# Seven half-block products in place of eight in the second FFN product of chunks 2 to 8 (sliding-window attention, then a gated FFN, one core)

## The chip, the core and the metric

The kernel runs on one core of a Trainium2 chip. The time is device microseconds of one execution. Before the change the median of three runs is 325.51 us (325.38 to 325.64). PE is TensorE's matmul, PEld its weight load, DVE VectorE, ACT ScalarE, POOL GpSimd, SP the engine whose queue issues most DMAs.

## What is computed

```
q, k, v: (8, 8, 576, 64)      # batch, heads, tokens, head width
scores = q k^T / 8, masked: heads 0-3 "plain" (0 <= i-j < 32),
         heads 4-7 "dilated" (0 <= i-j < 128 and (i-j) % 4 == 0)
attn   = softmax(scores) v    # (8, 8, 576, 64)
x      = attn, heads side by side: (4608, 512)
out    = (gelu(x w_gate) * (x w_val)) w_out      # d_ff = 1536, out (4608, 512), float32
```

## The kernel before

The FFN runs over 9 chunks c of 512 tokens. A chunk has two stages, and each is written out as a string of words (`gate_words`, `out_words`, lines 910 to 962) that `run_program` (L853) turns into instructions: the order on every engine's queue is the order of the words. A number n takes the next n matmuls from the stage's list.

*Gate stage.* For each of the 12 blocks nb of d_ff (128 wide) 4 matmuls of 512 columns for the gate and 4 for the value (`ffn1_part`, L623), into two PSUM banks; `g` (L872) is the gelu on ACT, `u` (L877) the product with the value on DVE, which reads the second bank, scales by USCALE and writes `u_all[:, nb]` in fp16. The banks alternate: 0 and 7 for even nb, 1 and 4 for odd. `firsts` (L970) gives the order of the first 16 matmuls by hand, since the xT of this chunk (the attention output, transposed, in four pieces kc) is only just ready. `F`, `H` and `R` load, cast (POOL) and turn (DMA transpose) q, k and v of a later batch; `e3` evicts the last output block of the chunk before.

*Output stage.* In chunks 0 to 6 the second product is plain (`ffn2`, L630): for each of 4 token blocks 12 matmuls of 128x512, in banks 0 and 7 alternately, each evicted by `w` (DVE, L643) or `e` (ACT, L641) with the scale 1/USCALE and sent by a DMA of SP (L645). Between these matmuls stands the attention of batch c+1, in four units i, j, k, l of two heads each: `S` scores (L458), `P` exp on ACT (L488), `M` mask on DVE (L493), `D` denominators and `N` numerators on PE (L458), `l` and `r` log and reciprocal on ACT (L585, L591), `X` the division on DVE, which writes xT (L614). S, D and N use stretches of banks 1 to 6 again and again, so each waits for the reader of what was there. `v0` and `v1` are POOL's casts of a later v (L254), held behind the masks. `E` and `G` load ACT's tables.

*Seven products.* In chunks 7 and 8 (`SEVEN`, L822) the second product is one level of a Strassen-like scheme: tokens in two halves, w_out's columns in two halves, and the 12 blocks of d_ff in 6 pairs give 2x2 blocks, and 7 products of such blocks replace 8. A product is 12 matmuls of 256 columns (`products`, L696). It needs sums of u (`u_sums`, L664 to 672, three per pair j: `k{j}@0` to `@2`) and of weights (`weight_sums`, L651 to 660, five per third of w_out, done in chunk 6: `K`). `part_out` (L708) takes a snapshot of the accumulating bank (q0, q1, q3 on ACT or DVE into `snap`) or an output block (q2, q4, q5, q6), and `part_sum` (L736 to 740) adds snapshots to each other, on POOL in chunk 7 and DVE in chunk 8. `last_products` (L747) does the last product of chunk 8 in three pieces.

Of the kernel before, what the change touches and what calls it, by code (L numbers as in the profile page):

```python
# [17 lines left out]
USCALE = 16.0  # L18
# [3 lines left out]
def kernel(  # L22
# [70 lines left out]
    t3s = [xT[i][:, 0:CH].rearrange("p (j d) -> p j d", j=2) for i in range(3)]  # L93
# [553 lines left out]
    def weight_sums(i, part):  # L647

        w = wo_t[i].rearrange("p (j k) (h d) -> p j k h d", k=2, h=2)
        b11, b12, b21, b22 = (w[:, :, k, h] for k in range(2) for h in range(2))  # L650
        if part == 0:  # L651
            nc.vector.tensor_tensor(wx[i][:, 0], b11, b22, ALU.add)
        elif part == 1:
            nc.vector.tensor_tensor(wx[i][:, 1], b11, b12, ALU.add)
        elif part == 2:
            nc.vector.scalar_tensor_tensor(wx[i][:, 2], b21, -1.0, b22, ALU.mult, ALU.subtract)
        elif part == 3:
            nc.vector.tensor_tensor(t3s[i], b12, b22, ALU.subtract)
        else:
            nc.vector.tensor_tensor(wx[i][:, 3], b21, b11, ALU.subtract)  # L660

    def u_sums(j, part):

        k0, k1 = u_all[:, 2 * j, :], u_all[:, 2 * j + 1, :]  # L664
        if part == 0:
            nc.vector.tensor_tensor(ux[:, j, 1:3].rearrange("p s t -> p (s t)"), k0, k1, ALU.add)
        elif part == 1:
            nc.vector.tensor_tensor(ux[:, j, 0], k0[:, 0:256], k1[:, 256:512], ALU.add)
        else:
            two = u_all[:, 2 * j : 2 * j + 2, :]  # L670
            flat = two.rearrange("p k t -> p (k t)")[:, 256:768].rearrange("p (k t) -> p k t", k=2)
            nc.vector.tensor_tensor(flat, two[:, :, 256:512], two[:, :, 0:256], ALU.subtract)

    def operands(kind):

        found = []
        for j in range(NKP):
            w = wo_t[j // 2][:, 2 * (j % 2) : 2 * (j % 2) + 2]
            x, k0, k1 = wx[j // 2][:, :, j % 2], u_all[:, 2 * j], u_all[:, 2 * j + 1]
            found.append(  # L680
                {
                    1: (ux[:, j, 0], x[:, 0]),
                    2: (ux[:, j, 2], w[:, 0, 0:HM]),
                    3: (k0[:, 0:256], t3s[j // 2][:, j % 2]),
                    4: (k1[:, 256:512], x[:, 3]),
                    5: (ux[:, j, 1], w[:, 1, HM:DM]),
                    6: (k0[:, 256:512], x[:, 1]),
                    7: (k1[:, 0:256], x[:, 2]),
                }[kind]
            )  # L690
        return found

    def products(bank, kind, first):

        return [
            lambda s=s, t=t, p=p, st=first and j == 0 and p == 0, end=j == NKP - 1: nc.tensor.matmul(  # L696
                ps[:, bank, HM * p : HM * p + HM], s[:, P * p : P * p + P], t, start=st, stop=end, skip_group_check=True
            )
            for j, (s, t) in enumerate(operands(kind))
            for p in range(2)  # L700
        ]

    def seven(banks):

        order = ((1, 3, True), (0, 4, True), (1, 5, False), (0, 1, False), (1, 2, True), (0, 7, False), (1, 6, True))
        return [mm for b, kind, first in order for mm in products(banks[b], kind, first)]

    def part_out(c, what, eng, banks):  # L708

        src, by = ps[:, banks[0 if what in (1, 3, 5) else 1], :], 1.0 / USCALE  # L710
        m3, a, f = snap
        dst = {0: m3, 1: a, 3: f}.get(what)
        osb = None
        if dst is None:
            osb = osbp.tile([P, DM], F32, tag="osb")
            dst = osb
        if what < 4:
            if eng:
                nc.scalar.activation(dst, src, AF.Copy, bias=0.0, scale=by)  # L719
            else:  # L720
                nc.vector.tensor_scalar(dst, src, by, None, ALU.mult)
        else:
            other, op = {4: (a, ALU.add), 5: (m3, ALU.subtract), 6: (f, ALU.add)}[what]
            nc.vector.scalar_tensor_tensor(dst, src, by, other, ALU.mult, op)  # L724
        if osb is not None:
            tiles["O", what] = osb
            t0, d0 = c * CH + 256 * (what in (4, 6)), HM * (what in (2, 6))
            dram = out[t0 : t0 + 256, d0 : d0 + HM].rearrange("(p r) d -> r p d", r=P)
            nc.sync.dma_start(out=dram, in_=osb.rearrange("r (p d) -> r p d", p=2))

    def part_sum(what, eng):

        m3, a, f = snap
        e = nc.vector if eng else nc.gpsimd
        if what == 0:
            e.tensor_tensor(f, f, m3, ALU.add)  # L736
        elif what == 1:
            e.tensor_tensor(m3, tiles["O", 2], m3, ALU.subtract)
        else:
            e.tensor_tensor(f, f, tiles["O", 4], ALU.subtract)  # L740

    def last_products(c):

        for p, c0, c1, bank in ((0, 0, HM, 3), (1, 0, P, 5), (1, P, HM, 6)):
            for j, (s, t) in enumerate(operands(6)):
                src = ps[:, bank, 0 : c1 - c0]
                nc.tensor.matmul(src, s[:, P * p : P * p + P], t[:, c0:c1], start=j == 0, stop=j == NKP - 1)  # L747
            osb = osbp.tile([P, DM], F32, tag="osb")
            dst, rest = osb[:, 0 : c1 - c0], snap[2][:, HM * p + c0 : HM * p + c1]
            nc.vector.scalar_tensor_tensor(dst, src, 1.0 / USCALE, rest, ALU.mult, ALU.add)  # L750
            t0 = c * CH + 256 + P * p
            (nc.scalar if c0 else nc.sync).dma_start(out=out[t0 : t0 + P, HM + c0 : HM + c1], in_=dst)
# [69 lines left out]
    SEVEN = range(7, NCH)  # L822
# [30 lines left out]
    def run_program(c, words, mms, banks):  # L853
# [3 lines left out]
        for word in words.split():  # L857
# [16 lines left out]
            elif kind == "u":  # L874
                nb = args[0]
                val = ps[:, gate_banks(c, nb)[1], :]
                nc.vector.scalar_tensor_tensor(u_all[:, nb, :], tiles.pop(("g", nb)), USCALE, val, ALU.mult, ALU.mult)  # L877
# [5 lines left out]
            elif kind == "K":  # L883
                weight_sums(*args)
            elif kind == "q":
                part_out(c, args[0], args[1], banks)
            elif kind == "s":
                part_sum(*args)
            elif kind == "L":
                mms.clear()  # L890
                last_products(c)
            elif kind == "V":
                (second, second_v)[args[0] if args else 0]()
            elif kind == "v":
                cast_part(c + 2, args[0], tiles["M"])
            elif kind == "F":
                load_first(args[0])
            elif kind == "H":
                load_rest(args[0])
            elif kind == "R":  # L900
                load_rest(3)
                load_first(4)
                load_rest(4)
            elif kind == "E":
                nc.scalar.preload_act_table_set("natural_log_exp_and_others")
            else:
                nc.scalar.preload_act_table_set("gelu_and_others")  # L907
        assert not mms

    def gate_words(c):  # L910
# [10 lines left out]
        if c in SEVEN:  # L921
            for j in range(NKP - 1):
                sums[2 * j + 1] += f" k{j}@0 k{j}@1 k{j}@2"
        if c == min(SEVEN) - 1:
            for i in range(3):
                for part in range(5):
                    sums[1 + (5 * i + part) * 2 // 3] += f" K{i}@{part}"
# [3 lines left out]
        before = f"e3@{c - 1}" if c < NCH - 1 and c - 1 not in SEVEN else ""  # L931
        last = f" u{NNB - 1} k5@0 k5@1 k5@2" if c > 6 else ""
        return f"{before} {loads} 7 G 3 g0 1 u0 1 g1 4 u1{sums[1]} {rest} 4 g{NNB - 1} 4{last}"

    def out_words(c):
# [6 lines left out]
        if c > 6:  # L942
            tail = "12 q6@0" if c < NCH - 1 else "L"
            return f"12 q0@1 12 q1@1 12 q2@0 12 q3@1 s0@{c - 7} s1@0 12 q4@0 s2@{c - 7} 12 q5@0 {tail}"
        i, j, k, l = (NHP * (c + 1) + n for n in range(NHP))
        v0, v1 = (" v0", " v1") if 2 < c < 6 else ("", "")
        if c in SEVEN:
            ahead = c > 2
            open_ = f"E P{i} P{j} 1 u11" if ahead else f"1 u11 7 S{i}@1+S{j}@4 E P{i} P{j}"
            after = f"S{l + 1}@12+S{l + 2}@15" if 1 < c < 6 else ""  # L950
            return (
                f"{open_} k5@0 k5@1 {11 if ahead else 4} q0@0 M{i} M{j}{v0} k5@2 12 q1@1 8 S{k}@1+S{l}@4 D{i}@11+D{j}@41 4 q2@0 "
                f"P{k} P{l} M{k} M{l}{v1} 12 q3@0 s0@0 s1@0 l{i} l{j} r{i} r{j} 12 q4@0 s2@0 N{i}@10+N{j}@40 D{k}@12+D{l}@42 "
                f"X{i} X{j} 12 q5@0 6 l{k} r{k} l{l} r{l} N{k}@13+N{l}@43 {after} X{k} 6 q6@0 X{l}"
            )
        first = f"1 u11 4 S{i}@1+S{j}@4 E P{i} P{j} M{i} M{j} 7 w0 5" if c < 3 else f"E P{i} P{j} 1 u11 M{i} M{j}{v0} 12 w0 3"
        after = f"S{l + 1}@12+S{l + 2}@15" if 1 < c < 6 else ""
# [12 lines left out]
    firsts = {c: orders[c if c < 3 else 2 if c == 3 else 3] for c in range(NCH)}  # L970
# [37 lines left out]
```

## Time and profile before

| | |
|---|---|
| median of 3 runs | 325.51 us |
| profiled execution | 325.92 us |
| its span, first to last instruction | 324.2 us |
| mean granted TensorE clock | 0.998 |
| gate stage of chunks 2 to 8, each (L623, 96 matmuls) | 20.72 us |
| output stage of chunk 2 / 3 to 5 / 6 / 7 | 14.07 / 13.3 / 12.91 / 9.17 us |

The page of the profile gives the busy time of each engine, the chain of work that ended last followed back from the end, and the costliest groups of instructions. In a row of the timeline or the groups stand start (us), duration (us), engine, line, operation, out<-in, shape, count, and in brackets the idle time of the engine before it and what ended it. A row of the chain has start, duration, engine, line and count. Matmul ends are modelled, and a row of several matmuls runs to the end of the last; neighbours overlap in it. A busy engine that nobody waits for costs nothing, so the chain is read first.

### The profile page before, as it was taken

The page shows a single profiled execution, that of the slowest core. Times are in us where ns is not written, and L with a number is a line of the kernel's source. Part 1 is how long each engine was busy: PE and PEld are TensorE (multiplying, and loading weights), DVE is VectorE, ACT ScalarE, POOL GpSimd, SP SyncE. Part 2 cuts the span into 40 slices and gives each one's busy share as a digit, 9 for nine tenths or more (in the row PEclk, how much of TensorE's full clock was granted, in tenths as well). Part 3 has the DMA queues.
Part 4 walks back from the last instruction along what each step waited for, and adds up shares of the span by engine and source line. Part 5 has one row for each costly group of instructions (what it writes and reads, how often), then busy time and mean ns, then how long its engine had stood idle before and what let it go on. Part 6 is the DMA issues. An engine that isn't in the chain of part 4 may idle for free.

```text
span 324.2 us, 7943 instructions
## 1 busy us (share of the span) xinstructions
PE 317.5 (98%) x3273; PEld 162.6 (50%) x3273; DVE 173.6 (54%) x287; ACT 159.1 (49%) x239; POOL 87.7 (27%) x138
## 2 busy tenths in 40 slices
PE   7999999999999999999999999999999999999995
PEld 4754544444544454445444454445444544684474
DVE  6764646435543355436543554446676467636654
ACT  2673567434653557347633764366535753333320
POOL 8785703402491422231124111411000000040001
PEclk9999999999999999999999999999999999999999
DMA  8999997998899898898389627973000210021003
GB/s 190 183 198 207 205 192 154 268 185 193 194 253 207 214 198 237 191 223 183 126 191 242 161 78 178 249 169 111 32 3 0 92 42 0 0 84 47 2 1 129
DMA packets 107700, 47.11 MB, mean 145 GB/s; under 512 B 83600, under 2 KB 104080, under 8 KB 107664
## 3 DMA queue, kind: packets, MB, share of 16 engines
q1 hardware_dynamic: 94160, 38.29, 51.1%
q0 software_dynamic: 12944, 7.67, 16.6%
q10 hardware_dynamic: 560, 0.66, 0.7%
q8 instruction: 25, 0.41, 0.5%
q14 instruction: 11, 0.09, 0.1%
HBM read 37.75 MB, written 9.44 MB: 146 GB/s over the span
## 4 chain that ended last, share of the span: by engine, by line
PE 92%; DMA 4%; DVE 1%; POOL 1%; issue 0%; DVEq 0%
PE ps L623 58%; PE ps L630 23%; PE ps L458 6%; PE ps L696 5%; DMA wg<-in_moe_w_gate_dram 2%; DMA xT<-in_q_dram 2%; POOL xT L182 0%; DVE turned L740 0%; PE ps L378 0%; DVE osb L724 0%; PE ps L398 0%; DVE osb L750 0%; POOL band L123 0%; DVE ones L67 0%; PE ps L447 0%
## 5 line engine op out<-in xcount | busy, mean ns | idle before, releaser
L877 DVE SCALAR_TENSOR_TENSOR u_all<-g,ps 128x512 f16<-128x512 f16 x108 | 74.2, 688 | 93.3 <-PE ps L623 76.2
L872 ACT ACTIVATE g<-ps 128x512 f16<-128x512 f32 x108 | 63.6, 597 | 105.3 <-PE ps L623 105.3
L623 PE MATMUL ps<-xT,wg 128*128 128x512 f16 x432 | 112.5, 379 | 0.2 <-DMA wg<-in_moe_w_gate_dram 0.2
L623 PE MATMUL ps<-xT,wv 128*128 128x512 f16 x432 | 112.3, 379 | 0.0
L630 PE MATMUL ps<-wo,u_all 128*128 128x512 f16 x336 | 77.8, 380 | 0.0
L623 PEld LDWEIGHTS <-wv 128*128 128x128 f16 x432 | 42.1, 98 | 51.0 <-DMA wv<-in_moe_w_val_dram 0.6
L623 PEld LDWEIGHTS <-wg 128*128 128x128 f16 x432 | 42.1, 98 | 50.5 <-DMA wg<-in_moe_w_gate_dram 0.3
L630 PEld LDWEIGHTS <-u_all 128*128 128x128 f16 x336 | 30.8, 98 | 35.6 <-issue 0.5
L614 DVE TENSOR_TENSOR xT<-ps,rb 128x576 f16<-128x576 f32 x32 | 28.7, 936 | 16.2 <-PE ps L458 12.9
L488 ACT ACTIVATE P<-ps 128x832 f16<-128x832 f32 (+1 forms) x32 | 25.3, 835 | 15.8 <-PE ps L458 15.7
L217 POOL CAST s<-stage 128x640 f16<-128x640 f32 x24 | 17.3, 747 | 53.5 <-DMA stage<-in_q_dram 38.9
L254 POOL CAST v<-stage 128x1152 f16<-128x1152 f32 x11 | 13.0, 1184 | 62.0 <-DMA stage<-in_v_dram 43.5
L585 ACT ACTIVATE lg<-ps 128x576 f32<-128x576 f32 x30 | 18.7, 653 | 11.4 <-DVE xT L614 8.8
L591 ACT ACTIVATE rb<-lg 128x576 f32<-128x576 f32 x30 | 19.5, 690 | 0.3
L736 POOL TENSOR_TENSOR turned<-turned,vdiag 128x512 f32<-128x512 f32 x1 | 1.3, 1262 | 65.6 <-ACT turned L719 65.6
L229 POOL CAST s<-stage 128x512 f16<-128x512 f32 x24 | 14.4, 629 | 8.6 <-DMA stage<-in_q_dram 6.7
L643 DVE TENSOR_SCALAR osb<-ps 128x512 f32<-128x512 f32 x21 | 14.4, 685 | 2.6 <-PE ps L630 2.0
L493 DVE TENSOR_TENSOR P<-P,two_p 128x832 f16<-128x832 f16 x14 | 8.6, 612 | 10.9 <-ACT P L488 10.9
L493 DVE TENSOR_TENSOR P<-P,two_d 128x768 f16<-128x768 f16 x14 | 9.1, 664 | 9.8 <-ACT P L488 9.2
L907 ACT ACT_TABLE_LOAD x9 | 11.5, 1283 | 0.2
L458 PEld LDWEIGHTS <-v 64*64 64x64 f16 x616 | 7.7, 107 | 6.2 <-issue 5.1
L458 PEld LDWEIGHTS <-q 64*64 64x64 f16 x576 | 7.9, 107 | 5.3 <-issue 3.7
(90 smaller groups left out, 208.0 us busy)
## 6 DMA issues: line engine op xcount, KB each, us to landing
out_dram<-osb SPq DMA_DIRECT2D x35, 256.0 KB, 2.2
stage<-in_v_dram SPq DMA_DIRECT2D x28, 144.0 KB, 3.6
stage<-in_q_dram SPq DMA_DIRECT2D x24, 128.0 KB, 3.6
stage<-in_k_dram SPq DMA_DIRECT2D x24, 128.0 KB, 2.9
stage<-in_q_dram SPq DMA_DIRECT2D x6, 512.0 KB, 5.1
stage<-in_k_dram SPq DMA_DIRECT2D x6, 512.0 KB, 5.3
stage<-in_v_dram SPq DMA_DIRECT2D x20, 128.0 KB, 2.9
wo<-in_moe_w_out_dram POOLq DMA_DIRECT2D x3, 512.0 KB, 16.2
```

Source lines behind the costliest of these rows:

```text
L217: nc.gpsimd.tensor_copy(s16[:, 1280 * t + 640 * g : 1280 * t + 640 * g + 640].rearrange("p (k c) -> p k c", k=5), st_of(i).rearrange("p (k ...
L458: nc.tensor.matmul(o[cols], lhs[rows], rhs[rows], start=st, stop=end, skip_group_check=True)
L488: nc.scalar.activation(pt[:, 0 : src.shape[1]], src, AF.Exp, bias=0.0, scale=scale)
L493: tiles["M"] = nc.vector.tensor_tensor(pt, pt, mask, ALU.mult)
L585: nc.scalar.activation(lg, psf[:, c0 : c0 + S], AF.Ln)
L591: nc.scalar.activation(rb, tiles.pop(("lg", n)), AF.Exp, scale=-1.0)
L614: nc.vector.tensor_tensor(dst, num, rb, ALU.mult)
L623: nc.tensor.matmul(ps[:, bank, :], w[:, kc, ns], xT[kc][:, tok], start=first, stop=end)
L630: nc.tensor.matmul(ps[:, bank, :], u_all[:, fc, tb * P : (tb + 1) * P], wo_t[fc // 4][:, fc % 4, :], start=(fc == 0), stop=(fc == NNB - 1),)
L696: lambda s=s, t=t, p=p, st=first and j == 0 and p == 0, end=j == NKP - 1: nc.tensor.matmul(ps[:, bank, HM * p : HM * p + HM], s[:, P * p : ...
L872: nc.scalar.activation(g, ps[:, gate_banks(c, args[0])[0], :], AF.Gelu)
L877: nc.vector.scalar_tensor_tensor(u_all[:, nb, :], tiles.pop(("g", nb)), USCALE, val, ALU.mult, ALU.mult)
```

## The change

The seven products are used in chunks 2 to 8 instead of 7 and 8. They follow another scheme of the same kind: product 1 (first in order) takes u and w_out as they are, there are four sums of u per pair in three operations (the first writes two), of which those after the first can cover two pairs at once, four sums of weights per third, and the snapshots are no longer added to each other: q0, q1, q2 are snapshots, q3, q4, q5 evictions that add one snapshot, q6 a plain eviction. u of odd blocks is stored negated in these chunks and USCALE is 8. The fourth weight sum lies in `wx` rather than in a free part of xT. Weight sums are made in chunk 1.

```
-USCALE = 16.0
+USCALE = 8.0
...
+    def u_sums(j, part, n=1):
+        lo, hi = slice(0, 2 * P), slice(2 * P, 4 * P)
         if part == 0:
+            k0 = u_all[:, 2 * j, :].rearrange("p (h t) -> p h t", h=2)
+            nc.vector.tensor_tensor(ux[:, j, 0:2], k0, u_all[:, 2 * j : 2 * j + 2, hi], ALU.subtract)
+            return
+        at = slice(j - n + 1, j + 1)
+        k0, k1 = (u_all.rearrange("p (j k) t -> p j k t", k=2)[:, at, k] for k in range(2))
+        if part == 1:
+            nc.vector.tensor_tensor(ux[:, at, 2], k0[:, :, lo], ux[:, at, 1], ALU.subtract)
         else:
+            nc.vector.tensor_tensor(k0[:, :, hi], ux[:, at, 2], k1[:, :, lo], ALU.subtract)
...
+    ORDER = ((0, 1, True), (1, 7, True), (0, 6, False), (1, 4, False), (0, 5, False), (1, 2, True), (0, 3, False))
...
+        if what in (3, 4, 5):
+            add = snap[{3: 2, 4: 1, 5: 0}[what]]
+            nc.vector.scalar_tensor_tensor(dst, src, -by if what == 5 else by, add, ALU.mult, ALU.add)
+        elif eng:
+            nc.scalar.activation(dst, src, AF.Copy, bias=0.0, scale=by)
+        else:
+            nc.vector.tensor_scalar(dst, src, by, None, ALU.mult)
+        if final:
+            sent(c, what, dst)
```

(`dst`, `src` and `add` with their reshapes left out here.) `ORDER` gives the place (0 or 1 of the stage's two banks), the product and whether it opens the bank: in chunks 2 to 6 place 0 is bank 0, place 1 bank 7. So q0, q2, q4, q6 read bank 0 and q1, q3, q5 bank 7, and each product but the fresh ones adds to a bank that the eviction before it must have read. `sent` issues the DMA of one 256x256 block, from SP unless told otherwise.

The last chunk gets a function of its own, in which products 1, 6, 5 and 3 go to two banks (one for each half of 128 tokens), 7 and 4 to a third, and the end is in pieces:

```
+        run(two, 1, True)
+        part_out(c, 0, 1, both)
+        run(z, 7, True)
+        part_out(c, 1, 1, 5)
+        run(two, 6, False)
+        part_out(c, 2, 1, both)
+        run(z, 4, False)
+        part_out(c, 3, 0, 5)
+        run(two, 5, False)
+        part_out(c, 4, 0, both)
+        run([(6, 0)], 2, True, parts=((0, 0, 256),))
+        piece(5, c11, ps[:, 6, 0:HM], 0, 0, 256)
+        run([None, (4, 0)], 2, True, parts=((1, 0, 128),))
+        piece(5, c11, ps[:, 4, 0:P], 1, 0, 128)
+        for p in range(2):
+            run(two, 3, False, parts=((p, 0, 256),))
+            piece(6, c12, ps[:, 2 + p, 0:HM], p, 0, 256, act=True)
+        run([None, (0, -P)], 2, True, parts=((1, P, 256),))
+        piece(5, c11, ps[:, 0, 0:P], 1, P, 256, q=nc.scalar)
```

The words (a number is matmuls; in `q0@1` the 1 stands for ACT, 0 for DVE; `k1@1@2` covers two pairs):

```
-    SEVEN = range(7, NCH)
+    SEVEN = range(2, NCH)
...
+                sums[2 * j + 1] += f" k{j}@0" + (f" k{j}@1@2 k{j}@2@2" if j % 2 else " k4@1 k4@2" if j == 4 else "")
...
+        before = "" if c == NCH - 1 else f"q6@1@{c - 1}" if c - 1 in SEVEN else f"e3@{c - 1}"
+        first = "7 G 1 g0 2 u0 4 g1 2 u1" if c - 1 in SEVEN and c < NCH - 1 else "7 G 3 g0 1 u0 1 g1 4 u1"
...
+            return "12 q0@1 12 q1@1 12 q2@1 12 q3@0 12 q4@0 12 q5@0 12 q6@1" if c < NCH - 1 else "L"
...
+            if c == 2:
+                open_ = f"1 u11 k5@0 7 S{i}@1+S{j}@4 E P{i} P{j} k5@1 4 q0@0 k5@2 M{i} M{j} 12 q1@1 6"
+            else:
+                open_ = f"E P{i} P{j} 1 u11 k5@0 k5@1 11 q0@0 k5@2 M{i} M{j}{v0} 12 q1@1 8"
             return (
+                f"{open_} S{k}@1+S{l}@4 D{i}@11+D{j}@41 P{k} P{l} {6 if c == 2 else 4} q2@0 M{k} M{l}{v1} 12 l{i} l{j} r{i} r{j} q3@0 "
+                f"12 N{i}@10+N{j}@40 D{k}@12+D{l}@42 q4@0 X{i} l{l} X{j} l{k} r{l} r{k} 12 q5@0 {8 if c == 2 else 4} "
+                f"N{k}@13+N{l}@43 {after} X{l} X{k} {4 if c == 2 else 8}"
             )
...
+    orders[4] = "012 013 112 113 002 003 001 000 011 010 102 103 101 100 111 110"
+    orders[5] = "010 011 110 111 000 001 003 002 013 012 100 101 103 102 113 112"
+    firsts = {c: orders[c if c < 3 else 3 if c == NCH - 1 else 4 if c == 3 else 5] for c in range(NCH)}
```

`q6` of chunks 2 to 6 stands at the head of the next chunk's gate stage, where `e3` stood, with its output DMA ahead of that stage's loads. A word of `orders` is block, gate (0) or value (1), and kc: the new orders begin with the value matmuls of blocks 0 and 1, in banks 7 and 4, and reach bank 0 with the fifth. Chunks 0 and 1 keep their words but for the weight sums in chunk 1's gate stage.

More of the change, by code (lines that the diff above doesn't have):

```diff
@@ L691, in operands @@
         return found
[L693 to L697, printed above, removed]
-            )
[L699 to L718, printed above, removed]
+    def products(banks, kind, first, parts=((0, 0, 256), (1, 0, 256))):
+        mms = []
+        for j, (s, t) in enumerate(operands(kind)):
+            opened = set()
+            for p, c0, c1 in parts:
+                bank, at = banks[p]
+                o = ps[:, bank, at + c0 : at + c1]
+                st, end = first and j == 0 and bank not in opened, j == NKP - 1
+                opened.add(bank)
+                mms.append(
+                    lambda o=o, s=s[:, P * p : P * p + P], t=t[:, c0:c1], st=st, end=end: nc.tensor.matmul(
+                        o, s, t, start=st, stop=end, skip_group_check=True
+                    )
+                )
+        return mms
@@ new lines, with seven, sent @@
+    ORDER = ((0, 1, True), (1, 7, True), (0, 6, False), (1, 4, False), (0, 5, False), (1, 2, True), (0, 3, False))
+    def seven(banks):
+        return [mm for b, kind, first in ORDER for mm in products([(banks[b], 0), (banks[b], HM)], kind, first)]
+    def sent(c, what, tile, p=slice(0, 2), cols=slice(0, 256), eng=None):
+        t0, d0 = c * CH + 256 * (what in (3, 4)), HM * (what in (4, 6))
+        dram = out[t0 : t0 + 256, d0 : d0 + HM].rearrange("(p r) d -> r p d", r=P)
+        (eng or nc.sync).dma_start(out=dram[:, p, cols], in_=tile.rearrange("r (p d) -> r p d", p=2)[:, p, cols])
@@ new lines, in part_out @@
+    def part_out(c, what, eng, src):
+        src, by = ps[:, src, :] if isinstance(src, int) else src, 1.0 / USCALE
+        final = what > 2
+        dst = osbp.tile([P, DM], F32, tag="osb", name="part") if final else snap[what]
+        if what in (3, 4, 5):
+            add = snap[{3: 2, 4: 1, 5: 0}[what]]
+            nc.vector.scalar_tensor_tensor(
+                dst.rearrange("r (p d) -> r p d", p=2) if len(src.shape) > 2 else dst,
+                src,
+                -by if what == 5 else by,
+                add.rearrange("r (p d) -> r p d", p=2) if len(src.shape) > 2 else add,
+                ALU.mult,
+                ALU.add,
+            )
+        elif eng:
+            nc.scalar.activation(
+                dst.rearrange("r (p d) -> r p d", p=2) if len(src.shape) > 2 else dst, src, AF.Copy, bias=0.0, scale=by
+            )
+        else:
+            nc.vector.tensor_scalar(dst, src, by, None, ALU.mult)
+        if final:
+            sent(c, what, dst)
@@ L719, in part_out, with last_chunk, run, piece @@
+    def last_chunk(c):
+        by = 1.0 / USCALE
+        two = [(2, 0), (3, 0)]
+        both = ps[:, 2:4, 0:HM]
+        z = [(5, 0), (5, HM)]
+        def run(banks, kind, first, **kw):
+            for mm in products(banks, kind, first, **kw):
+                mm()
+        def piece(what, osb, src, p, c0, c1, act=False, q=None):
+            dst = osb[:, HM * p + c0 : HM * p + c1]
+            if act:
                 nc.scalar.activation(dst, src, AF.Copy, bias=0.0, scale=by)
             else:
[L721 to L752, printed above, removed]
+                nc.vector.scalar_tensor_tensor(dst, src, -by, snap[0][:, HM * p + c0 : HM * p + c1], ALU.mult, ALU.add)
@@ new lines, in piece @@
+            sent(c, what, osb, slice(p, p + 1), slice(c0, c1), q)
+        run(two, 1, True)
[8 more added lines that the diff above has]
+        part_out(c, 4, 0, both)
+        c11 = osbp.tile([P, DM], F32, tag="osb", name="c11")
+        c12 = osbp.tile([P, DM], F32, tag="osb", name="c12")
+        run([(6, 0)], 2, True, parts=((0, 0, 256),))
@@ L885, in run_program @@
             elif kind == "q":
-                part_out(c, args[0], args[1], banks)
-            elif kind == "s":
-                part_sum(*args)
+                what, eng, at = (args + [c])[:3]
+                part_out(at, what, eng, out_banks(at)[what in (1, 3, 5)])
             elif kind == "L":
                 mms.clear()
-                last_products(c)
+                last_chunk(c)
             elif kind == "V":
@@ L930, in gate_words @@
             return f"{loads} 8 G 3 g0 1 u0 3 g1 1 u1{sums[1]} {rest} 4 g{NNB - 1} 4"
-        before = f"e3@{c - 1}" if c < NCH - 1 and c - 1 not in SEVEN else ""
+        before = "" if c == NCH - 1 else f"q6@1@{c - 1}" if c - 1 in SEVEN else f"e3@{c - 1}"
         last = f" u{NNB - 1} k5@0 k5@1 k5@2" if c > 6 else ""
-        return f"{before} {loads} 7 G 3 g0 1 u0 1 g1 4 u1{sums[1]} {rest} 4 g{NNB - 1} 4{last}"
+        first = "7 G 1 g0 2 u0 4 g1 2 u1" if c - 1 in SEVEN and c < NCH - 1 else "7 G 3 g0 1 u0 1 g1 4 u1"
+        return f"{before} {loads} {first}{sums[1]} {rest} 4 g{NNB - 1} 4{last}"
     def out_words(c):
```

50 lines of the change are left out of this document (15 added, 35 removed).

## The prediction

> **What bounds the kernel now.** I read the page first (busy shares, chain by engine), then the chain of waits in order of time, the windows of single stages, and the timeline around the hand-overs of PSUM banks.
>
> ```profile
> span 324.2 us, 7943 instructions
> PE 317.5 (98%) x3273; PEld 162.6 (50%) x3273; DVE 173.6 (54%) x287; ACT 159.1 (49%) x239; POOL 87.7 (27%) x138
> PE 92%; DMA 4%; DVE 1%; POOL 1%; issue 0%; DVEq 0%
> ```
>
> TensorE is busy for 98% of the span and 92% of the chain is its own work, so what counts is how long TensorE's list of matmuls is and whether anything makes it wait. The chain gives chunk 5 as one gate stage and one output stage; then come the last attention block of chunk 6 and chunk 7's output stage, which has the seven products already:
>
> ```profile
> 192.78 20.72 PE ps L623 x96
> 213.50 3.45 PE ps L630 x16
> 216.96 0.85 PE ps L458 x64
> 217.81 2.91 PE ps L630 x13
> 220.72 0.87 PE ps L458 x63
> 221.60 3.13 PE ps L630 x14
> 224.72 0.90 PE ps L458 x79
> 225.62 1.19 PE ps L630 x5
> ...
> 258.75 0.50 PE ps L458 x43
> ...
> 281.16 9.17 PE ps L696 x84
> ```
>
> No piece of another engine stands between these rows: the output stage of chunk 5 (13.31 us) is matmuls throughout. A full-width matmul costs 20.72/96 = 215.8 ns, a half-width one 9.17/84 = 109.2 ns. The L630 rows add up to 10.68 us for 48 matmuls against 48 x 215.8 = 10.36; the other 0.32 is the restart after three attention blocks, about 0.11 each (2.91 - 13 x 0.2158).
>
> ```profile
> 213.50:226.81 13.31, 13.31 (x258) 6.85 (x256) 7.59 (x12) 8.98 (x13) 2.29 (x2) 1.00 0.49 134
> 192.78:213.50 20.72, 20.72 (x98) 9.37 (x96) 8.45 (x12) 9.14 (x15) 5.41 (x9) 1.00 0.81 195
> ```
>
> The columns are sum, PE, PEld, DVE, ACT, POOL, granted clock, DMA share, GB/s. The granted clock is full. VectorE has 7.6 of 13.3 us in the output stage and 8.5 of 20.7 in the gate stage. So the change can gain only by shortening TensorE's list, and can lose it again where VectorE or ScalarE, which get more to do, empty a bank late.
>
> **The shorter list.** In chunks 2 to 6 the 48 full-width matmuls of a chunk (10.36 us) become 84 half-width ones (9.17 us): 1.19 us less. Attention blocks and restarts are as many as before. Five chunks: -5.95 us. Chunks 7 and 8 have the 84 already.
>
> **Sums of u and of weights.** The first row is a sum over 128x512, the second the weight loads of the half-width matmuls, the third, from the timeline, the last u of chunk 5:
>
> ```profile
> L666 DVE TENSOR_TENSOR ux<-u_all 128x512 f16<-128x512 f16 x12 | 5.1, 425 | 0.4
> L696 PEld LDWEIGHTS <-u_all 128*128 128x128 f16 x84 | 8.2, 98 | 1.4
> ...
> 213.61 0.69 DVE L877 SCALAR_TENSOR_TENSOR u_all<-g,ps 128x512 f16<-128x512 f16 x1 [1.04 <-PE ps L623]
> ```
>
> In a gate stage of chunks 2 to 6 come five sums k@0, four over two pairs each, and two half-size ones; at 0.42 us each at most 4.6 us, so VectorE has 8.45 + 4.6 = 13.1 of 20.72 us. Each u is needed only when its bank is filled again a block later, so I take nothing; if this cover were gone, a late u would stop the next gate matmul for as long as it is late. The twelve weight sums move from chunk 6 to chunk 1, where VectorE has the same twelve products of u. Even at the 0.69 us of a u they add 8.3 us to about 8.5: under 20.7, so nothing, as is their absence from chunk 6. POOL's casts run in these gates, and this is where I weigh a collision. In chunk 3:
>
> ```profile
> 150.62 1.97 DVE L493 TENSOR_TENSOR P<-P,two_d 128x768 f16<-128x768 f16 x2 [1.24 <-ACT P L488]
> 150.62 1.56 POOL L254 CAST v<-stage 128x1152 f16<-128x1152 f32 x1 [8.10 <-DMA stage<-in_v_dram]
> ```
>
> Two mask products, each with both inputs in SBUF, start together with a cast and take 1.97 us; both engines suffer. The page "SBUF — State Buffer", section "Who interferes with whom", of the Trainium skill calls this an exclusive lock of a shared port pair: a VectorE instruction with two SBUF inputs and a GpSimd instruction that reads SBUF keep each other out for a whole instruction. By that rule each sum can wait for one whole cast; the trace's pair agrees. In the gates POOL is busy 5.41 us, so even if the sums waited for all of it VectorE would reach 18.5 of 20.72 us; still nothing.
>
> **The output stages, walked through.** Rows of chunk 5 for what stays, of chunk 7 and its ScalarE copy for what comes:
>
> ```profile
> 213.34 3.62 PE L630 MATMUL ps<-wo,u_all 128*128 128x512 f16 x16
> ...
> 214.58 1.62 ACT L488 ACTIVATE P<-ps 128x832 f16<-128x832 f32 x2
> 216.24 0.59 DVE L493 TENSOR_TENSOR P<-P,two_p 128x832 f16<-128x832 f16 x1 [0.16 <-ACT P L488]
> 217.72 1.51 ACT L488 ACTIVATE P<-ps 128x768 f16<-128x768 f32 x2 [1.52 <-PE ps L458]
> 221.68 1.42 DVE L614 TENSOR_TENSOR xT<-ps,rb 128x576 f16<-128x576 f32 x2 [1.26 <-PE ps L458]
> 225.53 2.16 DVE L614 TENSOR_TENSOR xT<-ps,rb 128x576 f16<-128x576 f32 x2 [1.58 <-PE ps L458]
> ...
> 280.99 1.47 PE L696 MATMUL ps<-xT,u_all 128*128 128x256 f16 x12
> 282.56 0.60 ACT L719 ACTIVATE vdiag<-ps 128x512 f32<-128x512 f32 x1 [1.64 <-PE ps L696]
> 287.80 0.69 DVE L724 SCALAR_TENSOR_TENSOR osb<-ps,vdiag 128x512 f32<-128x512 f32 x1 [1.93 <-PE ps L696]
> ```
>
> An eviction starts 0.10 us behind the end of the last matmul (282.56 - 282.46), that is 0.37 behind that matmul's start, and takes 0.60 (ScalarE) or 0.69 (VectorE). Let t = 0 be the stage's first matmul (213.34 now). TensorE's new list: product 1 to t = 1.31, product 7 to 2.62, eight of product 6 to 3.49, S and D block with restart to 4.45, rest of 6 to 4.89, product 4 to 6.20, 5 to 7.51, N and D block to 8.49, 2 to 9.80, four of 3 to 10.24, N and S block to 11.25, eight of 3 to 12.12. VectorE in its order: u11 0.27 to 0.96, the sums k5@0 and k5@1 to 1.75, q0 to 2.44, k5@2, the mask products at about 2.8 to 4.0 (their P is there at 2.05 and 2.86), q2 5.15 to 5.84, two mask products until 6.9 (P comes 0.93 behind the S block, 0.76 apart, so the last at 5.93), q3 to 7.6, q4 7.77 to 8.46, two X from 8.64 (1.13 us behind the N block, as at 221.68) to 10.06, q5 to 10.75, two X from 11.22 to 13.38.
>
> Who waits for each: product 6 needs bank 0 back from q0 at 2.62 (0.18 to spare); the D matmuls need the masks at about 4.0 (none to spare for the last of them, which come later in the block); product 5 needs q2 at 6.20 (0.36); 2 needs q3 at 8.49 (0.9); 3 needs q4 at 9.80 (1.3); the second N block needs both X at 10.3 (0.2). In the next gate, bank 4 is wanted by its third matmul (12.55, X ends 12.30), the last quarter of xT by its eighth (13.63; 13.38). Those are short margins, yet all positive. q1 on ScalarE comes behind the two P (2.9 to 3.5; needed at 4.89). Three places go wrong by this reckoning:
> - q6 on bank 0 starts 0.37 behind the last matmul's start, at 12.38, and ends at 12.98; the gate's fifth matmul wants bank 0 at 12.12 + 4 x 0.2158 = 12.98. With a hand-over of 0.04 to 0.1 us (a mask product starts 0.04 behind its P, at 216.24) that is 0.06 at the gates of chunks 3 to 7: +0.3 in all (bounds 0 and 0.5).
> - Chunk 3: the v cast comes from DMA at 150.62 whatever TensorE does, and the stage starts 1.2 us earlier, so it still falls on the second pair of mask products. They end 0.7 us late, q3 and q4 follow, and the second N block waits about 0.3 (bounds 0 and 0.7).
> - Chunk 6 has a block of 0.50 in place of 0.90 before the gate, so bank 4 is wanted at 12.15 and is free at 12.35: +0.2, of which 0.06 is counted: +0.1 (0 to 0.3).
>
> Half-width reads over two banks, sums over two pairs, and rows of 1 KB in the output DMAs have no row among attention; the nearest (q's 0.60 and 0.69, sums of 0.42) leave them inside these bounds. On SP's queue each chunk has four output DMAs as before, and the next chunk's loads stand behind q6's as they stood behind the last store.
>
> **The tail.** Now:
>
> ```profile
> 318.36 1.24 DVE L740 TENSOR_TENSOR turned<-turned,osb 128x512 f32<-128x512 f32 x1
> 318.74 1.49 PE L747 MATMUL ps<-wx,u_all 128*128 128x256 f16 x18
> 320.12 0.82 DVE L750 SCALAR_TENSOR_TENSOR osb<-ps,turned 128x256 f32<-128x256 f32 x3
> 320.98 0.38 ACTq L752 DMA_DIRECT2D out_dram<-osb  x1
> ```
>
> Matmuls end at 320.23, but VectorE is held up by the slow sum of snapshots and ends at 320.94. The new tail has the same matmuls (twelve of them 128 wide), no sum, and behind the last a single 128x128 piece: 320.23 + 0.10 + 0.28 (a third of 0.82) = 320.61, the DMA at 320.64: -0.34 (bounds -0.4 and 0).
>
> **Sum.** -5.95 - 0.34 + 0.3 + 0.3 + 0.1 = -5.6. The profiled execution took 325.92 us (324.2 of span and 1.72 around it): 320.3, with a span of 318.6. It is 0.41 above the median of the runs, 325.51, so the prediction is **319.9 us**.
>
> **The rivals.**
> *Evictions late all over.* VectorE's output stage grows to 7.6 + 5 x 0.69 + 3 x 0.42 - 3 x 0.69 = 10.2 us of 12.1, in a fixed order; the margins at q0, the masks and X are 0.2 us or less. If each of these three slips 0.2 us further in every stage, 0.6 x 5 = 3.0 comes back: 322.9. For it: the short margins. Against: ends of the walk where VectorE waits for TensorE (before q2, q4, X) absorb a slip. Chance 0.20.
> *Half-width pairs don't keep their pace (slower).* A weight load takes 98 of the 109.2 ns, so a load stretched by DMA or POOL traffic would set the pace. With the other terms (+0.36) the kernel is slower than now from 122.5 ns a pair on; at 130 ns each stage has 10.92 us for 10.36: 5 x 0.56 + 0.36 = +3.2, 328.7. For it: chunk 7's 109.2 was seen without loads or casts beside it. Against: in chunk 5's gate, with a DMA share of 0.81 and casts, a load takes 9.37/96 = 98 ns too. Chance 0.04. The page "TensorE: Matmul & The Clock Gate", section "Back-to-back issue gap", of the Trainium skill speaks for it: streams of load and matmul are said to sustain 81 ns at 128 columns and 131 at 512, so half the width would cost well over half. By that, with an estimate of 106 ns midway, a stage would go from 6.3 to 8.9 us; the trace's 215.8 and 109.2 disagree with both figures.
> *The prefetch becomes the bound.* Stages end 1.2 us sooner each, loads don't.
>
> ```profile
> 142.64 2.05 SPq L272 DMA_TRANSPOSE q<-s x1
> 157.03 0.54 PE L458 MATMUL ps<-q 64*64 64x96 f16 x36
> ```
>
> In chunk 3 the last turned q or k is issued by 144.69 and read 12.3 us later; the gain of two chunks takes 2.1 of it. If it bound, it would give back those chunks' gain: 323. Chance 0.03. That nothing comes of it (the matmuls issued otherwise than written: 325.5): 0.02.
>
> **How the numbers follow.** The walk as made: 0.71; the rivals 0.20, 0.04, 0.03, 0.02. Its own range is 319.2 (no waits: 325.51 - 5.95 - 0.34) to 321.0 (all upper bounds: 319.2 + 1.5, and 0.3 if the tail gains nothing). The first rival reaches 322.9; taking in most of it, and 0.2 below for the spread of the runs, gives 319.0 to 322.5. About 0.2% (0.65 us) is what a measurement can tell from none; faster than that: the walk, the first rival and the prefetch, 0.93 with a little off; same 0.02; slower 0.05.
>
> **What would show it.** Five output stages with 84 half-width matmuls at 109.2 ns, each about 12.1 us long (12.9 in chunk 2, 11.7 in chunk 6); VectorE near 10.2 us in them; TensorE's idle time under 1 us in all, on q6 at the gates, on masks or X in chunk 3; a tail with ScalarE's DMA about 0.4 us behind the last matmul. A pace above 115 ns, or waits of TensorE on q0, masks or X in every stage, would prove it wrong.

## The result, and the profile after

The changed kernel takes 319.42 us (median of 4 runs, 319.24 to 320.22) against 325.45 for the kernel before beside it: 0.9816 of the time, 95% interval 0.9802 to 0.9829. That is 6.0 us less; forecast were 319.9 and 5.6. The profiled execution took 319.59 us, with a span of 317.9.

The page of the changed kernel, the lines that answer to those of before:

```profile
span 317.9 us, 8361 instructions
PE 311.8 (98%) x3453; PEld 180.3 (57%) x3453; DVE 203.3 (64%) x352; ACT 163.4 (51%) x247; POOL 83.8 (26%) x134
PE 95%; DMA 2%; ACT 1%; DVE 1%; POOL 1%; issue 0%
```

TensorE has 180 more matmuls and is still busy for 98%: the list became shorter and no idle time came in its place. VectorE has 30 us more to do. The chain of waits, chunk 5's output stage, and then chunk 7's gate stage:

```profile
210.01 3.49 PE ps L704 x32
213.50 0.85 PE ps L457 x64
214.36 3.16 PE ps L704 x28
217.52 0.88 PE ps L457 x63
218.39 1.85 PE ps L704 x16
220.25 0.89 PE ps L457 x79
221.14 0.98 PE ps L704 x8
...
254.56 20.80 PE ps L622 x96
```

The four L704 rows add up to 9.48 us for 84 matmuls, in place of 10.68 for 48; the attention blocks are as they were. The stage takes 12.11 us (13.31 before). As before, no row of another engine stands between them. The one gate stage that grew is chunk 7's, 20.80 for 20.72. Stage by stage, from the starts of the gate stages: chunks 2 to 6 gave 1.12, 1.19, 1.17, 1.20 and 1.19 us, 5.87 together.

The windows of chunk 5's output and gate stage (sum, PE, PEld, DVE, ACT, POOL, granted clock, DMA share, GB/s):

```profile
210.01:222.12 12.11, 12.11 (x293) 10.31 (x292) 9.28 (x17) 9.42 (x14) 2.29 (x2) 1.00 0.52 138
189.29:210.01 20.72, 20.72 (x98) 9.42 (x97) 14.26 (x24) 9.26 (x15) 5.92 (x9) 1.00 0.86 201
```

VectorE went from 7.6 to 9.3 us in the output stage and from 8.5 to 14.3 in the gate stage, and in this execution no wait of TensorE for it shows in chunks 2 to 8, apart from 0.08 us at chunk 7's gate. Chunk 2 has less room than this shows: when the same kernel was profiled again (e11_changed below), its output stage took 13.32 us, not 12.95. The chain of that run goes through the last u, the k5 sums, q0 and the first two mask products on VectorE. POOL was casting beside them, and the two half-size sums took 0.64 and 0.74 us (at 111.76 and 113.04), where chunk 5 has 0.29 and 0.28. TensorE's block starts behind the masks, after a wait of 0.3 us:

```profile
113.78 1.47 DVE P L492 x2
115.28 0.55 PE ps L457 x14
```

Three places of the walk are worth a look. First the gate after chunk 5's output stage, where q6 hands over bank 0:

```profile
221.06 2.16 DVE L613 TENSOR_TENSOR xT<-ps,rb 128x576 f16<-128x576 f32 x2 [0.48 <-PE ps L457]
221.07 1.05 PE L704 MATMUL ps<-wo,u_all 128*128 128x256 f16 x8
...
222.16 0.60 ACT L738 ACTIVATE part<-ps 128x512 f32<-128x512 f32 x1 [1.03 <-PE ps L704]
...
222.82 1.03 PE L622 MATMUL ps<-xT,wg 128*128 128x512 f16 x4
```

The matmuls end at 222.12, q6 runs from 222.16 to 222.76, and the gate's fifth matmul starts at 222.82, which is 4 x 215.8 ns behind its first (221.96): on time, 0.06 us behind the end of q6. Second, chunk 3, where a cast was to fall on the mask products:

```profile
143.69 2.63 SPq L271 DMA_TRANSPOSE q<-s  x2
...
149.87 1.02 DVE L492 TENSOR_TENSOR P<-P,two_d 128x768 f16<-128x768 f16 x2
...
153.05 1.15 POOL L253 CAST v<-stage 128x1152 f16<-128x1152 f32 x1 [8.38 <-DMA stage<-in_v_dram]
...
154.92 0.54 PE L457 MATMUL ps<-q 64*64 64x96 f16 x36
```

The cast came at 153.05, not at 150.62: loads and turns were themselves later in this execution, and the masks were over (1.02 us for two, 1.97 before). The last turn's issue is over at 146.32, and its result is read at 154.92: 8.6 us of room, where there were 12.3. Third, the tail:

```profile
311.64 2.80 PE L704 MATMUL ps<-wo,u_all 128*128 128x256 f16 x30
...
314.47 0.29 DVE L762 SCALAR_TENSOR_TENSOR c<-ps,vdiag 128x128 f32<-128x128 f32 x1 [1.36 <-PE ps L704]
314.79 0.38 ACTq L720 DMA_DIRECT2D out_dram<-c  x1
```

The last piece starts 0.03 us behind the last matmul's end (314.44) and the DMA follows 0.35 behind it; before, it was 0.75.

### The profile page after: what moved, and what is told of

It is laid out like the page before. It is cut to its first block, busy times and chain, and to the rows that moved or that the text cites. A ratio compares the mean times of both kernels' runs of the same rounds, so it can differ in the third digit from the quotient of the medians.

```text
span 317.9 us, 8361 instructions
## 1 busy us (share of the span) xinstructions
PE 311.8 (98%) x3453; PEld 180.3 (57%) x3453; DVE 203.3 (64%) x352; ACT 163.4 (51%) x247; POOL 83.8 (26%) x134
## 4 chain that ended last, share of the span: by engine, by line
PE 95%; DMA 2%; ACT 1%; DVE 1%; POOL 1%; issue 0%
PE ps L622 59%; PE ps L704 21%; PE ps L629 7%; PE ps L457 6%; DMA xT<-in_k_dram 2%; PE ps L377 1%; ACT P L487 1%; DVE xT L613 0%; PE ps L446 0%; POOL xT L181 0%; PE ps L796 0%; PE ps L397 0%; ACT rb L590 0%; POOL band L122 0%; PE ps L374 0%
## 5 line engine op out<-in xcount | busy, mean ns | idle before, releaser
L704 PEld LDWEIGHTS <-u_all 128*128 128x128 f16 x342 | 32.1, 98 | 5.6 <-issue 0.2
L487 ACT ACTIVATE P<-ps 128x832 f16<-128x832 f32 (+1 forms) x32 | 25.3, 834 | 12.4 <-PE ps L457 12.3
L704 PE MATMUL ps<-wo,u_all 128*128 128x256 f16 (+1 forms) x258 | 30.9, 271 | 0.0
L704 PE MATMUL ps<-wx,ux 128*128 128x256 f16 x252 | 30.7, 273 | 0.0
L704 PEld LDWEIGHTS <-ux 128*128 128x128 f16 x252 | 24.2, 98 | 3.3
L629 PE MATMUL ps<-wo,u_all 128*128 128x512 f16 x96 | 22.4, 380 | 0.0
L665 DVE TENSOR_TENSOR ux<-u_all 128x512 f16<-128x512 f16 x42 | 20.0, 476 | 1.5
L228 POOL CAST s<-stage 128x512 f16<-128x512 f32 x24 | 15.3, 666 | 7.1 <-DMA stage<-in_q_dram 6.0
L629 PEld LDWEIGHTS <-u_all 128*128 128x128 f16 x96 | 8.7, 98 | 9.8 <-issue 0.3
L670 DVE TENSOR_TENSOR ux<-u_all,ux 128x512 f16<-128x512 f16 (+1 forms) x28 | 12.0, 428 | 1.0
```

The source lines that it names most:

```text
L487: nc.scalar.activation(pt[:, 0 : src.shape[1]], src, AF.Exp, bias=0.0, scale=scale)
L629: nc.tensor.matmul(ps[:, bank, :], u_all[:, fc, tb * P : (tb + 1) * P], wo_t[fc // 4][:, fc % 4, :], start=(fc == 0), stop=(fc == NNB - 1),)
L665: nc.vector.tensor_tensor(ux[:, j, 0:2], k0, u_all[:, 2 * j : 2 * j + 2, hi], ALU.subtract)
L704: lambda o=o, s=s[:, P * p : P * p + P], t=t[:, c0:c1], st=st, end=end: nc.tensor.matmul(o, s, t, start=st, stop=end, skip_group_check=True)
```

## The experiments

The theory: the gain is the shorter list of matmuls, 1.19 us a stage, plus the tail; sums and evictions hide. The rivals: other edits gave part of it; half-width pairs keep their pace only in places; evictions or sums cost waits that are near.

**The eighth product put back (e1_eight).** Product 1 is done twice in chunks 2 to 6; all else stays as changed.

```
-        return [mm for b, kind, first in ORDER for mm in products(...)]
+        return [mm for b, kind, first in ORDER[:1] + ORDER for mm in products(...)]
...
-   k5@0 k5@1 11 q0@0          (chunk 2: 4 q0@0)
+   k5@0 k5@1 23 q0@0          (chunk 2: 16 q0@0)
```

> The changed kernel with product 1 done twice in chunks 2 to 6, so that each of these output stages has 96 half-width matmuls again; the second pass opens the bank anew and gives the same values. Sums, evictions, orders and tail stay as changed. Theory (the gain is the shorter list of matmuls, and sums and evictions are covered): 5 x 12 x 109.2 ns = 6.55 us come back, 319.4 + 6.55 = 326.0, stages of 13.4 us in chunks 3 to 5. Rival (a good part of the gain comes from the other edits: tail, snapshots no longer added up, orders of the first matmuls): the 6.55 us come back in part only where matmuls hid other waits, so the time stays clearly below 325. Second rival (evictions cost waits that more matmuls would hide): the time rises by less than 6 us.

Measured: 325.93 us (ratio to the kernel before 1.0008, 0.9999 to 1.0017). With 12 more half-width matmuls a stage the whole gain is gone: 6.5 us come back by the medians, 6.2 by the ratios, of the 6.55 reckoned. The stages of chunks 3 to 5 took 13.4 us in its profile, as expected. What is left of the change is worth next to nothing: the tail gains some 0.4 us, and 96 half-width matmuls take 0.12 us a stage more than 48 full-width ones, 0.6 in five stages. The gain is the list.

**Half-width matmuls in the kernel before (e2_half).**

```
-            nc.tensor.matmul(ps[:, bank, :], u_all[...], wo_t[fc // 4][:, fc % 4, :], start=(fc == 0), ...)
+            for h in range(2):
+                nc.tensor.matmul(ps[:, bank, HM * h : HM * h + HM], u_all[...],
+                    wo_t[fc // 4][:, fc % 4, HM * h : HM * h + HM], start=(fc == 0 and h == 0), ...)
```

> The kernel before with each full-width matmul of the plain second product (chunks 0 to 6) as two half-width ones with the same weights loaded twice: 96 x 109.2 ns in place of 48 x 215.8 in seven stages. Theory (half-width pairs keep 109.2 ns beside attention, loads and casts too): +0.12 us a stage, +0.87 in all, 326.3. Rival (the load of weights sets the pace, half the width costs well over half): at 122.5 ns a pair and more, +1.4 us a stage or more, 335 and above.

Measured: 326.50 us against 325.63 beside it (ratio 1.0027, 1.0016 to 1.0037), +0.87 us. In its profile the output stages of chunks 1 to 6 grew by 0.1 us each (chunk 5: 13.42 for 13.30). Half the width costs about 109 ns also beside attention, casts and loads. The rival that ends on the slow side is out.

**Only the new tail (e6_tail_only), and the new stages in chunks 5 to 8 alone (e7_from5).**

```
-    SEVEN = range(2, NCH)
+    SEVEN = range(7, NCH)        # e7_from5: range(5, NCH)
```

(with the old orders of the first matmuls in chunks whose predecessor has the plain product)

> The new scheme of products, sums and evictions and the new last chunk, but in chunks 7 and 8 alone as before; chunks 2 to 6 with the plain second product and the old orders. Theory (only the tail is new here): 0.3 to 0.5 us less than the kernel before, 325.0 to 325.2, all behind the last matmul. Rival (the new scheme as such is faster, for instance without POOL's sums of snapshots): 324 or less.

> The new scheme in chunks 5 to 8 only, the plain product in chunks 0 to 4, new tail. Theory (each stage gives its 1.19 us by itself): 325.45 - 0.4 - 2 x 1.19 = 322.7. Rival (what is gained in one chunk is lost or gained in another, as by a load that binds across chunks 2 to 4): 322.0 or less, or 323.4 or more.

Measured: the tail alone 325.25 against 325.69 (0.9990, 0.9981 to 0.9999), -0.4 us; from chunk 5 on 323.12 against 325.63 (0.9919, 0.9901 to 0.9937), -2.5 where -0.4 - 2 x 1.19 = -2.8 was reckoned. The interval of the latter is 2.1 to 3.2 us, and in its profile the stages of chunks 5 and 6 took 12.11 and 11.72 us, as in the changed kernel. With all five stages it is -6.0. Each stage gives its share by itself, within the measurement.

**q6 on VectorE (e3_q6_dve).**

```
-        before = ... f"q6@1@{c - 1}" if c - 1 in SEVEN ...
+        before = ... f"q6@0@{c - 1}" if c - 1 in SEVEN ...
```

> The changed kernel with q6 of chunks 2 to 6, the last eviction of bank 0, on VectorE in place of ScalarE. Theory (the fifth matmul of the next gate stage wants bank 0 at once, and VectorE is still at the two last divisions X): in chunk 5 X ends 223.22, q6 would end about 223.9, and the matmul wanted the bank at 222.82, so about 1.1 us are lost at each of five gates (less behind chunk 2, where X ends earlier): 324 to 325. Rival (banks are handed over with room, the order of the first matmuls covers it): no change, 319.4.

Measured: 324.61 us, 5.2 more than the changed kernel. The timeline at the same gate:

```profile
224.64 2.15 DVE L613 TENSOR_TENSOR xT<-ps,rb 128x576 f16<-128x576 f32 x2 [0.48 <-PE ps L457]
...
226.72 0.68 DVE L742 TENSOR_SCALAR part<-ps 128x512 f32<-128x512 f32 x1
227.45 1.02 PE L622 MATMUL ps<-xT,wg 128*128 128x512 f16 x4 [0.89 <-DVE part L742]
```

q6 stands behind both X, ends at 227.40, and the matmul that wanted the bank at 226.40 starts at 227.45. The five gates behind such a stage grew by 0.85 to 1.20 us in this profile, 5.2 together. The margin at this hand-over is real and thin: one eviction on the engine that is still busy gives back most of the gain, though VectorE's mean share of the stage is 77%.

**Each sum of u twice (e4_sums_twice).**

```
-   k{j}@0 ... k{j}@1@2 k{j}@2@2 ... k4@1 k4@2
+   k{j}@0 k{j}@0 ... k{j}@1@2 k{j}@1@2 k{j}@2@2 k{j}@2@2 ... k4@1 k4@1 k4@2 k4@2
```

> The changed kernel with each of the eleven sums of u in the gate stages of chunks 2 to 8 done twice in a row (the second gives the same values). Theory (VectorE has room in the gate stage, 12.8 to 14.3 of 20.7 us busy): 4.6 to 5.5 us more fit in, no change, 319.3 to 319.8. Rival (the sums share a port with POOL's casts, VectorE and the loads behind the casts are near their limit in chunks 2 to 5): u comes late and TensorE waits, or scores wait for q and k; 1 us or more in each of these chunks, over 323.

Measured: 325.28 us (323.66 to 326.54 over ten runs), 5.9 more. The theory's expectation was wrong, the rival's came true. In the profiled execution (323.66 us) the gates of chunk 3, with casts, and chunk 6, without:

```profile
123.17:145.00 21.83, 21.16 (x101) 9.55 (x99) 18.02 (x33) 9.45 (x15) 8.54 (x11) 1.00 0.89 221
...
225.69:246.50 20.81, 20.81 (x99) 9.43 (x97) 16.32 (x35) 9.25 (x15) 0.00 (x0) 1.00 0.05 17
```

and in chunk 3, where it went:

```profile
138.41 1.80 POOL L216 CAST s<-stage 128x640 f16<-128x640 f32 x2 [3.18 <-DMA stage<-in_k_dram]
...
138.81 1.67 DVE L670 TENSOR_TENSOR ux<-u_all,ux 128x512 f16<-128x512 f16 x2
...
141.32 1.28 DVE L910 SCALAR_TENSOR_TENSOR u_all<-g,ps 128x512 f16<-128x512 f16 x2
...
142.06 1.02 PE L622 MATMUL ps<-xT,wv 128*128 128x512 f16 x4 [0.67 <-DVE u_all L910]
```

The casts take 1.80 us (1.39 before the change) and the two sums beside them 1.67 (0.89 in chunk 6's gate, where nothing is cast); two u come late in a row, and the matmul that needs their bank waits 0.67. From one gate start to the next, chunks 3, 4 and 5 took 34.54, 34.15 and 33.83 us against 32.8 in the changed kernel, chunk 6 32.73 against 32.44, and chunk 7 30.06 against 29.97. Whether casts or the bunch of six sums was at fault was tried with two more runs.

**Twice, but only in chunks 6 to 8 (e8_twice_late); twice everywhere, but spread (e9_twice_spread).**

```
 e8:  sums twice if c > 5, else once
 e9:  at = {1: "0@0", 3: "1@0", 4: "1@1@2", 5: "2@0", 6: "1@2@2", 7: "3@0", 8: "3@1@2 3@2@2", 9: "4@0", 10: "4@1 4@2"}
      # each of these twice behind the u of that block
```

> Sums of u in the gate stages done twice as in the run with all of them doubled, but in chunks 6, 7 and 8 alone, where POOL casts nothing. Theory A (what the doubled sums cost is POOL's casts locking sums out and being locked out): three gates of 0.1 us, 319.4 to 319.9. Theory B (six sums in a row between two u are too long by themselves, casts or not): a share by chunk of the 5.9 us of all seven, 3 x 0.8 = 2.5 us, 321.9.

> All sums of u in the gate stages of chunks 2 to 8 done twice, as in the run that took 325.28, but spread: no more than four between two u, where that run had six behind blocks 3 and 7. VectorE's work is the same. Theory A (VectorE has too little time in the stage as a whole once casts lock it out): still above 323.5. Theory B (it is the bunch: one u comes late, the mean share of the stage says nothing): 319.5 to 321.5.

Measured beside the changed kernel itself (e11_changed, 319.78; expected as below): e8 319.87, e9 323.74. Without casts the doubled sums cost 0.1 us by the medians, and 0.5 by the stages of e8's profile (0.1 in each of three gates, 0.2 in chunk 6's output stage). Spreading them gave back only some 1.5 of the 5.9, and in e9's profile the time is lost in the output stages instead (14.41, 13.31, 12.74 and 12.94 us in chunks 2 to 5), while the gates take 20.7 to 20.8. So it is mainly the stages with casts, as theory A has it, and to a smaller part the bunch. Loads run in the same stages, but they are not what stretches a sum: in chunk 5's gate of the changed kernel, with a DMA share of 0.86, a sum that meets no cast takes 0.42 us (at 198.24), one beside a cast up to 0.89 (at 200.48). In e9, chunk 3:

```profile
137.85 1.86 POOL L216 CAST s<-stage 128x640 f16<-128x640 f32 x2 [2.93 <-DMA stage<-in_k_dram]
137.86 1.27 DVE L672 TENSOR_TENSOR u_all<-ux,u_all 128x512 f16<-128x512 f16 x2
139.06 0.67 DVE L910 SCALAR_TENSOR_TENSOR u_all<-g,ps 128x512 f16<-128x512 f16 x1
139.66 1.35 POOL L228 CAST s<-stage 128x512 f16<-128x512 f32 x2
139.76 1.53 DVE L665 TENSOR_TENSOR ux<-u_all 128x512 f16<-128x512 f16 x2
```

Sums and casts beside each other take 1.27 and 1.53 us (two sums; 0.88 without a cast, at 136.29), while the u between them keeps its 0.67.

> The changed kernel itself again, on the chip of the three runs beside it: 319.2 to 319.9.

**Chunk 1 too (e5_chunk1, e10_chunk1_masks).** The profile says that a stage is as long as its matmuls, and chunk 1 still had 48 full-width ones.

```
-    SEVEN = range(2, NCH)
+    SEVEN = range(1, NCH)       # weight sums stay in chunk 1; chunk 1 takes chunk 2's words, chunk 2 the order of chunk 3
 e10, chunks 1 and 2:
-   4 q0@0 k5@2 M{i} M{j} 12 q1@1
+   4 q0@0 M{i} M{j} k5@2 12 q1@1
```

> The seven products in chunk 1 as well, with its words after those of chunk 2; the weight sums and the sums of u then share chunk 1's gate stage. Theory (a stage is as long as its matmuls, VectorE has room): 1.19 us less in one stage, minus some 0.2 for bank 4 at the next gate, so 318.3 to 318.7. Rival (VectorE in chunk 1's gate, 8.6 us of u, 5.3 of weight sums, 5 of sums of u and POOL's casts beside them, comes too late; or the prefetch, which the shorter stages leave less time, becomes the bound): 319.4 or more.

> The seven products in chunk 1 too, and in chunks 1 and 2 the mask products ahead of the sum k5@2 on VectorE. In the version without this the stage of chunk 2 took 13.31 us for the 12.95 of the changed kernel, waiting for masks that stood beside a cast (1.84 us for two). Theory (the wait is VectorE's order): 0.2 to 0.3 us less than that version, 0.8 to 1.0 less than the changed kernel run beside it. Rival (the wait is the cast's, whatever the order): no less than that version, about 0.6 below the changed kernel.

Measured: e5 319.00 (0.9798, 0.9779 to 0.9816), above the 318.3 to 318.7 expected; e10 318.51 (0.9785, 0.9771 to 0.9798), the changed kernel beside e10 319.78 (0.9816, 0.9803 to 0.9830). In e5 chunk 1's output stage gives its 1.19 us (12.49 for 13.68), but chunk 2's takes 13.31 for 12.95, and its masks stand beside a cast:

```profile
112.10 1.54 POOL L228 CAST s<-stage 128x512 f16<-128x512 f32 x2
112.22 1.84 DVE L492 TENSOR_TENSOR P<-P,two_d 128x768 f16<-128x768 f16 x2
```

With the masks ahead of a sum that nobody needs yet, that stage takes 12.98 us in e10's profile. That the order of VectorE did this is not shown. The two masks take 1.84 us beside a cast there too, and with the words of the changed kernel the same stage took 12.80 (e8), 12.95, 13.32 (e11) and 13.85 us (e3) in one profile each: the spread from execution to execution is wider than the difference. By the ratios e10 is 0.4 us below e5, and their intervals overlap. What is shown is that e10, the fastest version of the study, is about 1.0 us below the changed kernel run beside it, 0.9785 against 0.9816 with intervals that don't overlap.

## Why the prediction was right

*The bound.* TensorE's list: right. e1 gives the eighth product back and gets the old time; e2 shows the pace of half-width pairs in seven stages. Term by term the profile has -5.87 - 0.38 + 0.08 = -6.2 us where -5.6 was forecast (the two profiled executions differ by 6.3 us, the medians by 6.0). The list and the tail were sized right; the waits added to them, 0.7 us, were 0.6 too dear.

*The five stages, -5.95.* Measured -5.87.

*The tail, -0.34.* The last VectorE piece ends 0.38 us earlier behind the start of chunk 8's output stage (9.51 for 9.89 us), and e6 has -0.4 for the tail alone. Right, by the step that was given: the slow sum is gone and the DMA follows the last matmul.

*q6 at the gates, +0.3.* Measured 0. The term was mis-sized: I took 0.10 us from the end of a matmul to the start of an eviction, from chunk 7 of the kernel before, but it was 0.04 here (222.12 to 222.16), and 0.05 from an eviction to the matmul (e3: 227.40 to 227.45). 0.06 less put the hand-over just in time. That it is a place that counts was right (e3: +5.2 us).

*The cast in chunk 3, +0.3.* Measured 0, and both halves of the term failed. The cast does not come "from DMA at 150.62 whatever TensorE does": here it came 2.4 us later, after the masks. What sets its time stays open. The sums of u alone it can't be: in e6 and e7, which have no such sums up to there and the same words in chunks 0 to 3, it came at 153.06 and 149.89, and the changed kernel's two profiles have 153.05 and 150.16. It differs from one execution, or chip, to the next, so whether it meets the masks is luck. The price was wrong too, since in e11_changed the cast did fall on the masks, and the stage still took 12.11 us:

```profile
150.07 1.96 DVE L492 TENSOR_TENSOR P<-P,two_d 128x768 f16<-128x768 f16 x2
150.16 1.46 POOL L253 CAST v<-stage 128x1152 f16<-128x1152 f32 x1 [7.44 <-DVE turned L742]
...
153.15 1.41 DVE L613 TENSOR_TENSOR xT<-ps,rb 128x576 f16<-128x576 f32 x2
154.70 0.57 PE L457 MATMUL ps<-P,v 64*64 64x96 f16 x44
```

The masks end at 7.66 behind the stage's first matmul (144.37), where the walk has 6.9 + 0.7. But q3, q4 and the two X then take 2.61 us in a row (151.95 to 154.56), not the 0.69 + 0.69 + 1.42 = 2.80 of the rows that the walk used, and the second N block starts at 154.70, 10.33 behind the first matmul, as in the profile without the collision. The slip used up the room and no more.

*Bank 4 behind chunk 6, +0.1.* Measured 0.08: chunk 7's gate is the only one that grew, within its first four matmuls, before the one that wants q6's bank.

*Sums in the gates, nothing.* Right as forecast, and its reason holds: "even if the sums waited for all of it VectorE would reach 18.5 of 20.72 us". The same reckoning for doubled sums gives 18.5 + 4.6 = 23.1, more than the stage has; I left that out when I expected nothing of e4. Where casts run, the cover is thus one set of sums deep, not two. The page "SBUF — State Buffer", section "Who interferes with whom", of the Trainium skill has the rule behind it: a lock between a VectorE instruction with two SBUF inputs and a GpSimd instruction that reads SBUF. The runs agree as far as they go: sums and casts lengthen each other (0.88 to 1.53, 1.39 to 1.86), the u, with one input in PSUM, stays at 0.67 to 0.69, and without casts (e8) the cost nearly goes.

*Late evictions all over, 0.20.* Didn't occur all over. VectorE's work in the stage rose by 1.7 us (to 9.3), less than the 2.6 reckoned (10.2). In single executions VectorE did hold TensorE up where casts ran beside it: at the masks of chunk 2 in e11_changed (13.32 us for 12.95), and at q0 of chunk 3 in e8 (12.57 for 12.11, with the changed kernel's words). So the doubt about the short margins was sound there.

*The prefetch, 0.03.* Didn't bind, but 3.7 of 12.3 us of its room in chunk 3 are used up, more than the 2.1 that I gave it. In e11_changed's profile it is 1.6 (the last turn's issue is over at 144.42, its result read at 155.12), so this too differs by execution, and one profile can't size it.

## What to carry to other kernels

Where one engine is busy without a gap, price a change by what it takes off that engine's list, then walk the new stage once with each bank's hand-over and each engine's fixed order: the walk found a hand-over on which 5 us hang (e3), which the mean shares don't show, though the small waits that it added up did not come. Work "hidden" on another engine is hidden against a deadline and beside the other engines that stretch it; reckon how many times over it would still fit. A wait of some tenths of a us that hangs on when a load lands needs more than one profile. When a stage has proved to be as long as its matmuls, ask which other stage still has the long form.

## What was not expected of the hardware

From the end of the last matmul to an eviction it was 0.10 us in chunk 7 of the kernel before and 0.04 behind chunk 5's output stage in the changed one; why, the runs don't show. That sums and casts stretch each other was foreseen, the price was not: two sums with both inputs in SBUF, 0.88 us by themselves, took up to 1.67 beside casts (e4), and the casts grew from 1.39 to as much as 1.86 (e9). And the time at which a cast gets its data differed by some 3 us between two executions of the same program (153.05 and 150.16 in chunk 3).
